# Attention and two MoE layers on one core: tails of four heads in one load, second keys copied on the chip, tails summed in one step

## The chip, the cores and the metric

One core of a Trainium2 chip runs the whole program. The metric is the device time of one execution in microseconds (us); the number quoted is the median of several executions.

## What is computed

The reference is an attention layer, then a top-1 mixture of experts, then a soft mixture. B=4, H=8, S=576, D=64; 2304 tokens of 512 features go through 8 experts of width 1024, twice.

```python
scores = scale * q @ k.T ; causal ; a = softmax(scores) ; local = a @ v
q_p = phi(q)                                  # phi(x) = (x > 0 ? x : exp(x) - 1) + 1
mem_out = (q_p @ M_prev) / (q_p @ z_prev + 1e-6)
attn = g * mem_out + (1 - g) * local          # g = sigmoid(beta), one number a head
logits = x @ w_gate + modality_bias ; e = argmax(logits)
y = gate_w * (relu(x @ w1[e]) @ w2[e])        # then the soft mixture with 32 slots
```

## The kernel before

A head has 576 rows: four chunks of 128 and a tail of 64. The kernel works on 16 pairs p. A pair is the same head of two batches; its two tails of 64 rows share one chunk of 128, chunk 4, so a pair has nine chunks. A head is j = 2p + s, s the place in the pair (0 the even head, 1 the odd one).

Each pair goes through named steps. The names are the ones in the order table at the end of the file, with the line numbers of the profile:

- Loads. `Lk`, `Lq`, `Lv` (L108) load the eight whole chunks of a tensor with two DMAs of 128 KB, issued by SyncE (SP). `Tk`, `Tq`, `Tv` (L113) load the two tails with one DMA of 32 KB, issued by ScalarE (ACT). All goes into `raw`, which has two buffers.
- Splits. Keys, queries, values and phi(q) are split into a high and a low 16-bit part: `kh` (L170 ACT), `kl` (L173 GpSimd), `qh` (L176 ACT), `ql` (L180 VectorE, DVE), `pe` (L184 ACT, an exponential), `prl` (L188 ACT), `pm` (L192 DVE), `ph` (L195 ACT), `pl` (L198 DVE), `vh` (L201 ACT), `vl` (L204 DVE).
- `tr1` (L210, SP): a DMA transpose of keys and queries into `tt`. `k2` (L213, SP): a DMA that copies the high and low keys, 64 partitions x 1152, into `k2t`, of which three buffers are kept; the other 64 partitions hold -1, filled at the start (L121).
- Row maxima. `x0` to `x3` (PE, L225 to L238) multiply the high parts into a PSUM bank `mxp`, and `y0` to `y3` (DVE, L246 and L261) reduce them with the mask added. `x0` of the odd head also does the product of each tail with itself, 64x64, in two products (L230). `tr2` (L265, SP) transposes the maxima and low queries into `q2t`.
- Scores. `S0` to `S3` (PE, L279, L280, L283), then the exponentials `E0` to `E3` (L301 ACT) into `e`, and the low part `el` by `l0` to `l3` (L307 GpSimd). `e` and `el` have two buffers, one for the even and one for the odd head.
- Value sums. `A0` to `A3` (L334 PE) sum a chunk of 128 rows over its key chunks, four products for each (two parts of e by two of v), 65 columns: 64 of values and the row sum. `A4` of each head does the tail: 16 products on 128 rows and, for the tail with itself, four on 64 rows.
- Memory. `M` (L357, L358 PE), `mc`, `mr` (L363, L367 DVE), `mx` (L374 ACT, writes `x_all`). `mL`, `mA` and others prepare the matrices of 8 heads at a time (L151 SP loads `mr`, L157 ACT rounds it to `mh`).
- Norms. `Na` (L384 DVE) takes the row sums of the head's bank; for the odd head a second instruction of one column takes the shared tail, which lies in the even head's bank. `Nb` (L388), `N` (L396 DVE, adds into `x_all`).

The routing of the MoE is worked in chunks among the attention steps: (half, k) with half 0 or 1 and k 0 to 3. `cT` transposes (L551 PE), `cX` copies to SBUF (L558 DVE for g = 1, L560 ACT), `cM` multiplies with the gate weights (L565 PE, one product for each g of 0, 1, 2, into 32 rows of one bank each; float32, two records in the trace for one product), `cC` adds up (L571 or L573 DVE). The last chunk (1, 3) is done in the start of the MoE part (L1176 to L1182). `r1` (L578) and the further steps make the indices. `s00` to `s11` store tokens (L669, L671 SP), `pf` loads the first expert's weights (L1692), `ga` gathers rows (L1695 GpSimd).

The order of all this is written out by hand: `PLACES` gives each step an offset, the period is 10 a pair, pairs 0, 1, 2, 14 and 15 have corrections, and the steps are sorted by `offset + 10 p` and emitted in that order. Each engine runs its instructions in the order in which they were emitted; a wait at one holds all that stand behind it on the same engine.

```python
todo = [(offs[n] + period * p + offs.get(f"{n}@{p}", 0), f"{n}@{p}", lambda f=f, p=p: f(p)) for n, f in steps.items() for p in range(NP)]
todo += [(offs[n], n, f) for n, f in once.items()]
with tc.manual_schedule():
    fills()
    for _, n, f in sorted(todo, key=lambda t: t[:2]):
        f()
```

## Time and profile before

| | us |
|---|---|
| median of three runs | 597.95 |
| lowest and highest run | 597.41, 601.11 |
| profiled execution, its time | 601.41 |
| profiled execution, its span | 599.7 |
| busy in the span: PE, DVE, ACT, GpSimd | 519.3, 347.0, 256.9, 216.7 |

The profiled execution is one run of its own: its time is 3.46 us above the median, and 1.7 us of it lie outside the span that the trace covers. The attention takes up to some 240 us of the span; the rest is the two MoE layers. A busy time counts instructions at work; an engine whose busy share is close to one in a stretch has little room there. Rows with a bracket at the end, `[idle before <-releaser]`, say how long the engine stood idle before the instruction and what released it.

### The profile page before, as it was taken

Reading aid. Unit: us, or ns where it says so; the run is one execution under the profiler, and the core shown is the slowest. Engines: PE = TensorE matmul, PEld = TensorE weight load, DVE = VectorE, ACT = ScalarE, POOL = GpSimd, SP = SyncE. Lnnn points to the kernel's source line nnn. Section 1 sums busy time; section 2 is a strip of 40 time slices with the busy share of each in tenths; the row PEclk is TensorE's granted clock in tenths of the full one; section 3 lists DMA queues with packets and bytes.
Section 4 is the critical chain, followed back from the end, with each engine's and each line's share of the span. In section 5 each row is a group of like instructions: output and inputs, shape, how many; then the busy total and the mean of one; then the engine's idle time right before and its main releaser. Section 6 shows DMA issues by size and latency. Waiting matters only on the chain. (4 is left out here: it accounts for less than half of the span.)

```text
span 599.7 us, 17104 instructions
## 1 busy us (share of the span) xinstructions
PE 519.3 (87%) x6421; PEld 349.4 (58%) x6421; DVE 347.0 (58%) x1194; ACT 256.9 (43%) x580; POOL 216.7 (36%) x277
## 2 busy tenths in 40 slices
PE   0368889999999999659699999998999899789993
PEld 0146656766776868226667667674666567465342
DVE  4668889999988998398542433435443232422233
ACT  4348668777777856252422212423321122210033
POOL 5155656666765757145743210212112111101000
PEclk9998989999999999798899999998999899976998
DMA  5999899999999859893568656761438778585988
GB/s 104 166 175 185 171 183 193 169 175 184 167 165 189 172 120 134 211 213 122 147 192 201 199 178 213 248 179 39 132 91 182 237 235 227 165 314 184 345 261 292
DMA packets 194514, 111.85 MB, mean 187 GB/s; under 512 B 160262, under 2 KB 174543, under 8 KB 194400
## 3 DMA queue, kind: packets, MB, share of 16 engines
q1 hardware_dynamic: 181376, 91.97, 65.7%
q10 hardware_dynamic: 10528, 13.17, 7.7%
q0 software_dynamic: 2496, 5.32, 3.3%
q8 instruction: 54, 0.88, 0.6%
q14 instruction: 60, 0.49, 0.2%
HBM read 75.93 MB, written 9.91 MB: 143 GB/s over the span
## 5 line engine op out<-in xcount | busy, mean ns | idle before, releaser
L307 POOL TENSOR_TENSOR el<-e 128x512 f16<-128x512 f32 (+2 forms) x128 | 113.0, 903 | 71.8 <-ACT e L301 65.3
L1009 PE MATMUL ps_g<-xt,w1h 128*128 128x128 f16 x1088 | 98.7, 221 | 6.0 <-DMA xt<-xt 5.4
L1009 PE MATMUL ps_g<-xt,w1l 128*128 128x128 f16 x544 | 95.2, 221 | 0.2 <-issue 0.2
L1009 PEld LDWEIGHTS <-w1h 128*128 128x128 f16 x1088 | 84.7, 99 | 14.7 <-issue 11.7
L999 PE MATMUL ps_y<-w2h,hts 128*128 128x512 f16 (+1 forms) x288 | 89.2, 377 | 3.2 <-issue 3.2
L301 ACT ACTIVATE e<-sp 128x512 f32<-128x512 f32 (+2 forms) x128 | 62.9, 510 | 43.8 <-PE sp L280 16.5
L1061 POOL DMA_INDIRECT cbuf<-ce,gidx x17 | 17.7, 1042 | 162.1 <-DVEq L1396 89.7
L334 PE MATMUL avp<-vh,e 128*128 128x65 f16 (+2 forms) x480 | 74.4, 199 | 0.3 <-DVE x_all L396 0.3
L334 PE MATMUL avp<-vl,e 128*128 128x65 f16 (+2 forms) x480 | 72.8, 196 | 0.0
L334 PE MATMUL avp<-vl,el 128*128 128x65 f16 (+2 forms) x480 | 72.5, 195 | 0.0
L334 PE MATMUL avp<-vh,el 128*128 128x65 f16 (+2 forms) x480 | 72.2, 194 | 0.0
L334 PEld LDWEIGHTS <-e 128*128 128x128 bf16 (+2 forms) x960 | 62.5, 102 | 16.6 <-issue 10.6
L999 PEld LDWEIGHTS <-hts 128*128 128x128 f16 x432 | 43.4, 104 | 45.0 <-issue 4.0
L279 PE MATMUL sp<-tt 128*128 128x64 f16 (+4 forms) x288 | 59.9, 251 | 2.3 <-ACT e L301 2.2
L334 PEld LDWEIGHTS <-el 128*128 128x128 f16 (+2 forms) x960 | 61.8, 103 | 0.1
L280 PE MATMUL sp<-q2t,k2t 128*128 128x64 f16 (+4 forms) x288 | 57.0, 250 | 3.5 <-DMA q2t<-qs 3.5
L1016 ACT ACTIVATE hts<-ps_g 128x512 f16<-128x512 f32 x34 | 20.3, 597 | 84.6 <-PE ps_g L1009 84.6
L999 PE MATMUL ps_y<-w2l,hts 128*128 128x512 f16 (+1 forms) x144 | 54.1, 376 | 0.0
L1009 PEld LDWEIGHTS <-w1l 128*128 128x128 f16 x544 | 53.7, 99 | 0.0
L246 DVE CUSTOM_DVE_ANT_0 mxp<-mxp,mq 128x512 f32<-128x512 f32 (+1 forms) x64 | 39.5, 626 | 13.6 <-PE mxp L232 8.3
L1036 DVE COPY si<-ps 128x512 f32<-128x512 f32 x19 | 13.1, 689 | 51.7 <-PE ps L1034 51.7
L1017 DVE SCALAR_TENSOR_TENSOR hts<-ps_g,hts 128x512 f16<-128x512 f32 x34 | 23.5, 690 | 33.4 <-ACTq L1377 22.7
(410 smaller groups left out, 1139.4 us busy)
## 6 DMA issues: line engine op xcount, KB each, us to landing
va<-in_moe_w_dram SPq DMA_DIRECT2D x12, 1024.0 KB
va<-in_moe_w_dram ACTq DMA_DIRECT2D x9, 1024.0 KB
rw<-in_moe_w_dram SPq DMA_DIRECT2D x8, 1024.0 KB
va<-in_moe_w_dram SPq DMA_DIRECT2D x16, 512.0 KB
raw<-in_q_dram SPq DMA_DIRECT2D x32, 128.0 KB
raw<-in_k_dram SPq DMA_DIRECT2D x32, 128.0 KB
raw<-in_v_dram SPq DMA_DIRECT2D x32, 128.0 KB
rw<-in_moe_w_dram SPq DMA_DIRECT2D x2, 2048.0 KB
```

What stands on the lines that cost most here:

```text
L246: nc.vector.tensor_tensor_reduce(out=ps[:, src:src + n] if out is None else out, in0=ps[:, src:src + n], in1=msk, scale=1.0, scalar=-3.0e3 ...
L279: nc.tensor.matmul(ps[:, dst:dst + n], k1[:, ko:ko + 128], q1[:, qo:qo + n], start=True, stop=False)
L280: nc.tensor.matmul(ps[:, dst:dst + n], k2[:, ko:ko + 128], q2[:, qo:qo + n], start=False, stop=last)
L301: nc.scalar.activation(out=es[j % 2][0][:, a:a + n], in_=st.pop(("sp", j, g))[:, 0:n], func=AF.Exp, scale=0.125)
L307: nc.gpsimd.tensor_tensor(el[:, a:a + n], e[:, a:a + n], hv[:, a:a + n], op=ALU.subtract)
L334: nc.tensor.matmul(dst, l, r, start=(i == 0), stop=(i == len(mms) - 1))
L999: nc.tensor.matmul(ps, a[:, l, :], r, start=(start and j == 0), stop=(stop and j == 2))
L1009: nc.tensor.matmul(dst, l, r, start=(j == 0), stop=(j == len(mms) - 1))
L1016: nc.scalar.activation(out=hi, in_=ps, func=AF.Relu)
L1017: nc.vector.scalar_tensor_tensor(lo, ps, 0.0, hi, op0=ALU.max, op1=ALU.subtract)
L1036: nc.vector.tensor_copy(st["x2t"], tp)
L1061: ins = nc.gpsimd.indirect_dma_start(out=cbuf, out_offset=bass.IndirectOffsetOnAxis(ap=idx, axis=0), in_=ce, in_offset=None, bounds_check= ...
```

## The change

1. Tails. One load `U` for a tensor brings the tails of four pairs (a group g; two DMAs of 64 KB, issued by SP, with the 64 rows as the leading dimension) into one tile `tls`, which has a single buffer for each tensor. `Tk`, `Tq`, `Tv` become copies on ACT, 128x64, from `tls` into chunk 4 of `raw`. 24 DMAs take the place of 48; 48 copies are new.
2. `k2` becomes a copy on DVE, 64x1152; two buffers of `k2t` in place of three.
3. The two 64x64 tail products of `x0` become one of 128x128, whose mask has the two off-diagonal quarters closed; its reduction has 128 columns in place of 64.
4. `A40` and `A41` become one step `A4` a pair: 20 products for each head, all on 128 rows, the two heads taken in turn into the two halves of the columns, in the odd head's bank. The odd head's `Na` is one instruction in place of two. The even head's `e` and `el` are held until `A4`.
5. The three `cM` products of a chunk are issued behind one another, as one step; the third `xt` lies in a part of another tile.
6. `PLACES` is new throughout. At the start SP's order is `Uq0 Lq0 Lk0 Uk0 Lq1 Lk1 mL0 .. tr1@0 .. tr2@0` (before: `Lq0 Lk0 .. Lk1 Lq1 tr1@0 Lk2 mL0 Lv0 tr1@1 k2@0 Lq2 tr2@0`), and `mA0` stands behind `pe@1` and `kh@2` on ACT (before: ahead of `pe@1`). Pair 0's reductions stand almost together. The loads of group 1 stand behind `Lq4`, those of group 2 behind `Lk8`, `Uv2` ahead of `Lk10`, and those of group 3 around `Lk12`. At the end, the transposes of chunk (1, 2) lie among pair 15's steps, its products behind `A20@15` and its sum behind the last norm `N1@15`.

The diff, with the order table left out:

```diff
@@ -54,10 +54,6 @@
...
     c["mq"] = mq
-    mqt = const.tile([128, 64], BF16, name="mqt")
-    nc.vector.tensor_copy(mqt[0:64], mq[0:64, 384:448])
-    nc.vector.tensor_copy(mqt[64:128], mq[64:128, 448:512])
-    c["mqt"] = mqt
     zero = const.tile([128, 1], BF16, name="zero")
@@ -74,8 +70,9 @@
...
         NP = 16
-        NR, NSRC, NTT, NV, NK2, NQ2 = 2, 2, 5, 5, 3, 3
+        NR, NSRC, NTT, NV, NK2, NQ2 = 2, 2, 5, 5, 2, 3
         raws = [ap.tile([128, 3, 9, 64], F32, name=f"raw{i}") for i in range(NR)]
+        tls = ap.tile([128, 3, 4, 64], F32, name="tl")
         srcs = [ap.tile([128, 27, 128], F16, name=f"src{i}") for i in range(NSRC)]
@@ -86,7 +83,7 @@
...
-        junk = [junk[:, 0:128], junk[:, 128:384], junk[:, 384:448]]
+        junk = [junk[:, 0:128], junk[:, 128:384], junk[:, 384:512]]
         cfm = [ap.tile([128, 5], F32, name=f"cfm{i}") for i in range(2)]
@@ -96,6 +93,8 @@
...
         ml = ap.tile([128, B * H, 65], F16, name="ml")
+        mqt = ap.tile([128, 128], BF16, name="mqt")
         st = {}
@@ -108,11 +107,20 @@
...
-        def load_tails(p, i, t):
-            b0, h = 2 * (p // 8), p % 8
-            nc.scalar.dma_start(out=raws[p % NR][:, i, 4, :], in_=t[b0:b0 + 2, h, 512:576, :])
+        def load_tails(g, i, t):
+            b0, h = 2 * (g // 2), 4 * (g % 2)
+            for s in range(2):
+                nc.sync.dma_start(out=tls[64 * s:64 * s + 64, i], in_=t[b0 + s, h:h + 4, 512:576, :].rearrange("h r d -> r h d"))
+        def put_tails(p, i):
+            nc.scalar.activation(out=raws[p % NR][:, i, 4, :], in_=tls[:, i, p % 4, :], func=AF.Copy)
         def fills():
+            nc.gpsimd.memset(mqt, NEG)
+            for s in range(2):
+                d = slice(64 * s, 64 * s + 64)
+                nc.vector.tensor_copy(mqt[d, d], cs["mq"][d, 384 + 64 * s:448 + 64 * s])
             nc.gpsimd.memset(x_all[0:64, 0, :], 0.0)
@@ -210,7 +218,7 @@
...
         def k_again(p):
-            nc.sync.dma_start(out=k2s[p % NK2][0:64], in_=tts[p % NTT][0:64, 0:9, :])
+            nc.vector.tensor_copy(k2s[p % NK2][0:64], tts[p % NTT][0:64, 0:9, :])
@@ -225,9 +233,8 @@
...
                 if s == 1:
-                    for i in range(2):
-                        t = side(i)[1]
-                        nc.tensor.matmul(ps[64 * i:64 * i + 64, 384:448], q1[:, t:t + 64], k1[:, t:t + 64], start=True, stop=True)
+                    nc.tensor.matmul(ps[:, 384:512], q1[:, 512:640], k1[:, 512:640], start=True, stop=True)
             elif part == 1:
@@ -251,7 +258,7 @@
...
                 if s == 1:
-                    ttr(64, 384, 10, cs["mqt"], junk[2])
+                    ttr(128, 384, 10, mqt, junk[2])
             elif part == 1:
@@ -306,32 +313,33 @@
...
-        def av(j, c):
-            p, s = j // 2, j % 2
+        def av_terms(j, cols, n, base):
             e, el = es[j % 2]
             hv = e.bitcast(BF16).rearrange("p (n t) -> p n t", t=2)[:, :, 1]
-            vh, vl = vhs[p % NV], vls[p % NV]
-            a = j if c < 4 else j - s
-            if c == 0:
-                st["av", j] = ps_a.tile([128, 325], F32, name="avp", tag="av")
-            acc = st["av", a]
-            base = 5 * s
-            if c < 4:
-                cols = [128 * c, 512 + 128 * (c - 1), 960 + 128 * (c - 2), 1280 + 128 * (c - 3)][:c + 1]
-                n, dst = 128, acc[:, 65 * c:65 * c + 65]
-            else:
-                cols = [1472, 896, 1216, 1408, 1536]
-                n, dst = 64, acc[64 * s:64 * s + 64, 260:325]
-            mms = []
+            vh, vl = vhs[j // 2 % NV], vls[j // 2 % NV]
             for kc, a in enumerate(cols):
-                r = slice(0, 128) if kc < 4 else slice(64 * s, 64 * s + 64)
                 ch = base + kc if kc < 4 else 4
...
                     for rh in (vh, vl):
-                        mms.append((lh[r, a:a + n], rh[r, ch, :]))
+                        yield lh[:, a:a + n], rh[:, ch, :]
+        def av(j, c):
+            if c == 0:
+                st["av", j] = ps_a.tile([128, 325], F32, name="avp", tag="av")
+            dst = st["av", j][:, 65 * c:65 * c + 65]
+            cols = [128 * c, 512 + 128 * (c - 1), 960 + 128 * (c - 2), 1280 + 128 * (c - 3)][:c + 1]
+            mms = list(av_terms(j, cols, 128, 5 * (j % 2)))
             for i, (l, r) in enumerate(mms):
                 nc.tensor.matmul(dst, l, r, start=(i == 0), stop=(i == len(mms) - 1))
+        def av_tails(p):
+            acc = st["av", 2 * p + 1]
+            mms = [list(av_terms(2 * p + s, [1472, 896, 1216, 1408, 1536], 64, 5 * s)) for s in range(2)]
+            for i in range(20):
+                for s in range(2):
+                    l, r = mms[s][i]
+                    nc.tensor.matmul(acc[64 * s:64 * s + 64, 260:325], l, r, start=(i == 0), stop=(i == 19))
@@ -374,14 +382,10 @@
...
-        def banks(j):
-            return [(st["av", j], 0, 4)] + ([(st["av", j - 1], 4, 1)] if j % 2 else [])
         def norm_cf(j):
-            h = j // 2 % 8
-            for a, c0, n in banks(j):
-                nc.vector.tensor_scalar(cfa[j % 2][:, c0:c0 + n], wsum(a, 5)[:, c0:c0 + n], 1e-9, c1[:, h:h + 1], op0=ALU.add, op1=ALU.mult)
+            h, n = j // 2 % 8, 4 + j % 2
+            nc.vector.tensor_scalar(cfa[j % 2][:, 0:n], wsum(st["av", j], n), 1e-9, c1[:, h:h + 1], op0=ALU.add, op1=ALU.mult)
@@ -389,17 +393,16 @@
...
-            h = j // 2 % 8
-            for a, c0, n in banks(j):
-                for c in range(c0, c0 + n):
-                    xt = x_all[:, tiles(j, c), 64 * h:64 * h + 64]
-                    nc.vector.scalar_tensor_tensor(xt, a[:, 65 * c:65 * c + 64], cfa[j % 2][:, c:c + 1], xt, op0=ALU.mult, op1=ALU.add)
+            h, a = j // 2 % 8, st.pop(("av", j))
+            for c in range(4 + j % 2):
+                xt = x_all[:, tiles(j, c), 64 * h:64 * h + 64]
+                nc.vector.scalar_tensor_tensor(xt, a[:, 65 * c:65 * c + 64], cfa[j % 2][:, c:c + 1], xt, op0=ALU.mult, op1=ALU.add)
         steps = {"Lk": lambda p: load(p, 0, k), "Lq": lambda p: load(p, 1, q), "Lv": lambda p: load(p, 2, v),
-                 "Tk": lambda p: load_tails(p, 0, k), "Tq": lambda p: load_tails(p, 1, q), "Tv": lambda p: load_tails(p, 2, v),
+                 "Tk": lambda p: put_tails(p, 0), "Tq": lambda p: put_tails(p, 1), "Tv": lambda p: put_tails(p, 2),
                  "kh": k_hi, "kl": k_lo, "qh": q_hi, "ql": q_lo, "tr1": tr1, "pe": phi_e, "prl": phi_r,
                  "pm": phi_m, "ph": phi_hi, "pl": phi_lo, "vh": v_hi, "vl": v_lo, "k2": k_again,
-                 "tr2": tr2}
+                 "tr2": tr2, "A4": av_tails}
         for s in range(2):
@@ -408,7 +411,7 @@
...
                 steps[f"S{i}{s}"], steps[f"E{i}{s}"], steps[f"l{i}{s}"] = head(st_group, i), head(e_exp, i), head(e_lo, i)
-            for i in range(5):
+            for i in range(4):
                 steps[f"A{i}{s}"] = head(av, i)
@@ -417,6 +420,9 @@
...
                 once[f"{n}{i}"] = lambda f=f, i=i: f(i)
+        for g in range(4):
+            for i, (n, t) in enumerate((("k", k), ("q", q), ("v", v))):
+                once[f"U{n}{g}"] = lambda g=g, i=i, t=t: load_tails(g, i, t)
         period, offs = at
@@ -488,6 +494,9 @@
...
         self.place = pool.tile([128, NT, 128], BF16, name="place")
+        self.xt2 = self.place[:, 9:18].rearrange("p a b -> p (a b)").bitcast(F32)
+        self.fo = self.xt2[:, 384:384 + 9 * NE].rearrange("p (t e) -> p t e", e=NE)
+        self.xt2 = self.xt2[:, 0:384]
         self.iop = iof("iop", [128, 1], [[0, 1]], cm=1)
@@ -552,18 +561,19 @@
...
     def chunk_x(self, g):
-        xt = self.st["xt", g] = self.wk.tile([128, 384], F32, name="xt", tag="xt")
+        xt = self.st["xt", g] = self.xt2 if g == 2 else self.wk.tile([128, 384], F32, name="xt", tag="xt")
         xp = self.st.pop(("xp", g))
...
-    def chunk_m(self, k, g, bank):
-        if g == 0:
-            self.st["lp"] = bank()
-        self.nc.tensor.matmul(self.st["lp"][32 * g:32 * g + 32, 0:384], self.wg[:, k, :], self.st.pop(("xt", g)), start=True, stop=True,
-                              tile_position=(0, 32 * g))
+    def chunk_m(self, k, bank):
+        self.st["lp"] = bank()
+        for g in range(3):
+            self.nc.tensor.matmul(self.st["lp"][32 * g:32 * g + 32, 0:384], self.wg[:, k, :], self.st.pop(("xt", g)), start=True, stop=True,
+                                  tile_position=(0, 32 * g))
@@ -694,7 +704,7 @@
...
         sh = [128, 9, NE]
-        o = wk.tile(sh, F32, name="fo", tag="fo", bufs=1)
+        o = self.fo
         s = wk.tile([128, 9], F32, name="fs", tag="fs")
@@ -1176,8 +1186,7 @@
...
                 first_split(0, 0)
-                for g in range(3):
-                    rt.chunk_m(3, g, lambda: rot("ps_y", 2))
+                rt.chunk_m(3, lambda: rot("ps_y", 2))
                 rt.chunk_c(1, 3)
@@ -1710,7 +1719,7 @@
...
                 once[f"cX{half}{k}{g}"] = lambda g=g: rt.chunk_x(g)
-                once[f"cM{half}{k}{g}"] = lambda k=k, g=g: rt.chunk_m(k, g, lp_bank)
+            once[f"cM{half}{k}"] = lambda k=k: rt.chunk_m(k, lp_bank)
             once[f"cC{half}{k}"] = lambda half=half, k=k: rt.chunk_c(half, k)
```

## Rows read from the trace of the kernel before

**Rows 1.** Windows, 75 to 225 us: window, length, busy (x instructions) per engine, PEclk, DMA share, GB/s

```profile
75.00:225.00 150.00, 144.81 (x2405) 104.28 (x2401) 135.75 (x515) 110.72 (x278) 94.05 (x106) 0.99 0.95 172
```

**Rows 2.** DMA view, 75 to 225 us: queues by kind, then issues by line

```profile
q10 hardware_dynamic: 3900, 0.98, 3.2%
...
k2t<-tt SPq DMA_DIRECT2D x12, 144.0 KB
```

**Rows 3.** Waits, PE, 75 to 225 us: us in total, times, longest us

```profile
PE mxp L225 <- DVE qs L246: 2.0, 2, 1.7
```

**Rows 4.** Waits, DVE, 75 to 225 us: the first and last of nine on PE

```profile
DVE R L246 <- PE mxp L230: 2.9, 4, 1.2
...
DVE acc L571 <- PE lp L565: 0.2, 1, 0.2
```

**Rows 5.** Timeline, PE, from 125 us: start us, duration us, instruction

```profile
126.09 0.20 PE L334 MATMUL avp<-vl,e 128*64 128x65 f16 x1
...
126.53 0.20 PE L334 MATMUL avp<-vl,el 128*64 128x65 f16 x1
126.66 0.22 PE L334 MATMUL avp<-vh,e 64*64 64x65 f16 x1
...
126.97 0.27 PE L226 MATMUL mxp<-tt 128*128 128x256 f16 x1
127.17 0.22 PE L230 MATMUL mxp<-tt 128*64 128x64 f16 x2
127.33 0.20 PE L334 MATMUL avp<-vh,e 128*128 128x65 f16 x1
...
131.17 0.22 PE L357 MATMUL mmp<-mh,tt 128*64 128x65 f16 x2
131.22 0.20 PE L358 MATMUL mmp<-ml,tt 128*64 128x65 f16 x2
```

**Rows 6.** Windows, line L565 alone, 75 to 225 us

```profile
75.00:225.00 150.00, 15.65 (x36) 2.52 (x36) 0.99 0.95 172
```

**Rows 7.** Timeline, PE, 245 to 258 us

```profile
251.07 1.29 PE L565 MATMUL ps_y<-xt,wg 128*32 128x384 f32 x4
```

**Rows 8.** Timeline, SP, 120 to 150 us

```profile
120.89 0.52 SPq L213 DMA_DIRECT2D k2t<-tt  x1
```

**Rows 9.** Timeline, DVE, 222 to 300 us

```profile
243.33 0.86 DVE L396 SCALAR_TENSOR_TENSOR x_all<-avp,cfa,x_all 128x64 f32<-128x64 f32 x4 [4.64 <-remote]
...
268.85 0.37 DVE L787 TENSOR_SCALAR R<-R,iop 128x576 bf16<-128x576 bf16 x1
```

**Rows 10.** Groups by shape, 0 to 300 us: busy us, mean ns, idle before

```profile
L374 ACT ACTIVATE x_all<-mmp,cfm 128x64 f32<-128x64 f32 x144 | 32.9, 320 | 9.2 <-DVE cfm L367 8.9
...
L198 DVE TENSOR_TENSOR src<-pm,src 128x576 f16<-128x576 f32 x16 | 17.0, 1062 | 3.6 <-ACT src L195 3.6
...
L246 DVE CUSTOM_DVE_ANT_0 R<-mxp,mq 128x128 bf16<-128x128 f32 x32 | 8.9, 278 | 4.3 <-PE mxp L230 3.6 <-PE mxp L226 0.8
...
L246 DVE CUSTOM_DVE_ANT_0 R<-mxp,mqt 128x64 bf16<-128x64 f32 x16 | 3.5, 218 | 0.0
...
L384 DVE TENSOR_SCALAR cfa<-avp,c 128x1 f32<-128x1 f32 x16 | 3.3, 205 | 0.0
...
L121 DVE MEMSET k2t<- 64x1152 f16 x3 | 3.1, 1018 | 0.7 <-issue 0.5 <-DMA raw<-in_q_dram 0.2
```

**Rows 11.** Timeline, DVE, 0 to 44 us

```profile
25.66 0.76 DVE L198 TENSOR_TENSOR src<-pm,src 128x576 f16<-128x576 f32 x1
```

**Rows 12.** Timeline, PE, 0 to 75 us

```profile
33.34 0.37 PE L280 MATMUL sp<-q2t,k2t 128*128 128x256 f16 x1 [3.46 <-DMA q2t<-qs]
```

**Rows 13.** Timeline, SP, 0 to 44 us

```profile
12.14 2.81 SPq L210 DMA_TRANSPOSE tt<-src  x1
...
29.05 1.30 SPq L265 DMA_TRANSPOSE q2t<-qs  x1
```

**Rows 14.** Timeline, ACT, 0 to 44 us

```profile
22.91 0.64 ACT L157 ACTIVATE mh<-mr 128x520 f16<-128x520 f32 x1 [5.92 <-DMA mr<-in_M_prev_dram]
```

152 lines of the change are left out of this document (76 added, 76 removed).

## The prediction

> **What bounds the kernel now.** I read the page's 40 slices first: the first 16 (attention, up to some 240 us) are where the change lives, TensorE (PE) and VectorE (DVE) both near full there, with the granted clock at its upper level. The expert blocks behind are touched only by their start. So I took the steady middle, 75 to 225 us, as my sample. The reader is to see in [rows 1] that of 150 us PE is busy 144.81, DVE 135.75, ScalarE 110.72 and GpSimd 94.05, and that the DMA engines are 95% taken. Twelve pairs pass in it (12 issues of `k2t` in [rows 2]), so a pair costs 150 / 12 = 12.5 us. Who waits for whom: PE's largest wait for another engine is 2.0 us in all [rows 3], while DVE waits for PE in nine rows, from 2.9 down to 0.2 us, 11.6 us in sum, of its 150 - 135.75 = 14.25 us of idle time [rows 4]. So PE is the bound and DVE is next, about 10% behind. That decides how much of a saving on PE can reach the time: the room to DVE, less what the change gives DVE to do.
>
> **What the change takes from PE.** (a) The tail sums. A tail step of one head is 16 products on 128 rows at 0.031 us ((126.53 - 126.09) / 14), then a change of tile shape (126.53 to 126.66 = 0.13, that is 0.10 more than a product), four 64-row products and another change at its end [rows 5]. Two heads: 40 x 0.031 = 1.24 plus six changes of shape. After: 20 couples in the two halves of the columns and two changes. A couple in two halves starts 0.05 after the one before (131.17 to 131.22, two products each) [rows 5], so 20 x 0.052 = 1.04. Saved: 0.20 + 4 x 0.10 = 0.60 a pair. (b) The tail maxima: from L226 to the next step is 127.33 - 126.97 = 0.36; at 0.031 for 65 columns L226's 256 take 0.12, and one 128-column product in the shape of its neighbours would take 0.06. Saved 0.18. Together 0.78 a pair, 9.4 us in the twelve pairs.
> (c) The routing products. 18 of them (36 records) take 15.65 us, 0.87 each [rows 6]. The change issues the three of a chunk behind one another, into three column groups. Four records that stood together took 1.29 against 2 x 0.87 = 1.74 [rows 7], so they overlap; I take about 0.9 for three adjacent instead of 2.6, the low end, because each goes to its own columns as the couples in (a) do; the high end is 3 x 0.65 = 1.9. Saved 1.65 a chunk (0.7 at the high end), six chunks in the stretch: 9.6 us. PE's load in the stretch falls by 9.4 + 9.6 = 19.0 us. It can't all be had: DVE is 14.25 us away.
>
> **What it gives DVE.** The copy `k2` (64x1152, 16-bit) replaces a DMA issue of 0.52 us on SP [rows 8]. No DVE row shows it. Nearest below: a 128x576 pass of 16-bit data at 0.37 [rows 9], half the columns. Nearest above: the fill of the same tile, 64x1152, at 1.02 [rows 10], plus some 0.3 where it stands against GpSimd, for a pass over 576 columns takes 0.76 with GpSimd idle [rows 11] and 1.06 in the mean of sixteen [rows 10]. Ends 0.37 and 1.3; I take 0.7, twice the 16-bit row, since it is the same kind of pass. The tail maximum grows from 64 to 128 columns: 278 - 218 = 0.06 more; one 128x1 normaliser goes: 0.205 less [rows 10]. Net 0.7 + 0.06 - 0.205 = +0.56 a pair, +6.7 in the stretch: DVE at 135.75 + 6.7 = 142.5 busy. Of its idle time the waits for PE go down with PE's load, which I put at two thirds, 11.6 to 3.9; what else it waits for (14.25 - 11.6 = 2.65) stays. 142.5 + 3.9 + 2.65 = 149.0: **the steady stretch gains only 1 us**, and DVE becomes the bound.
> [...]
>
> **What it moves off the queues.** 48 tail DMAs leave ScalarE's queue (3.2% of the DMA time in the stretch [rows 2]); 48 copies of 128x64 come onto ScalarE. The nearest row, a 128x64 pass that reads PSUM, is 0.32 [rows 10]; 48 x 0.3 = 14 us over all attention, 10 in the stretch: 110.7 + 10 = 121 of 150, hidden beneath PE and DVE as long as nothing on DVE waits for the order of ScalarE (if that cover goes, it is a few tenths a pair). SP loses 16 issues of 0.52 and gets 24 of the kind, +5 us over 240: hidden, but in the start four of these stand ahead of the first transpose. The DMA engines lose the twelve `k2t` transfers and the small tail packets; they were not what PE waited for, so nothing.
>
> **The start.** The first score product waits until 33.34 for `q2t` [rows 12], whose transpose is issued at 29.05 behind the maxima of pair 0 [rows 13]. Between stands a stall: ScalarE idles 5.92 for `mr` before `mh` at 22.91 [rows 14], DVE waits behind it, and the maxima of pair 0 are split around it. After, the `mr` load is issued before pair 0's transpose and the reductions of pair 0 run together, which would end them some 4 us earlier; but four tail DMAs and the `mr` load (together some 2 us) stand ahead of the first transpose, which is issued at 12.14 now. Sum -2, bounds -5 and +2.
>
> **The end.** After the last norm the old order still has routing products, a transposed chunk and the sums on them (rows at 251.07 [rows 7]); in the new order the transposes of the chunk before last lie among the last pair's steps, its products before the last tail sums, and only one sum is behind the last norm. I take 3 products and a copy, -3 (bounds -5, -1.5). The four pairs outside the stretch and the start take a part of the PE saving where DVE is less full: 4 x 0.5 = -2.
>
> **Sum.** -1 - 2 - 3 - 2 = -8 us (stretch, start, end, other pairs). The profiled execution took 601.41, and DVE stood idle 4.64 us before the norm at 243.33 with nothing of its own core named as releaser [rows 9]; I count this as an accident of that execution, neither gained nor lost, and the median 597.95 lies 3.46 below it. From the median: 597.95 - 8 = **590**.
>
> **The rivals.**
> 1. *The copy is cheap and PE's saving comes through* (0.2). With 0.37 a copy DVE's net is +0.23 a pair, 135.75 + 2.7 = 138.5; if its PE waits vanish, 138.5 + 2.65 = 141.1, -8.9 in the stretch, -7 elsewhere: 597.95 - 15.9 = **582**. For it: PE's 19.0 is more than all DVE's idle time. Against: the new order's waits needn't vanish.
> 2. *The copy eats it* (0.17). At 1.3 DVE gets +1.15 a pair, 13.8: 149.6 busy plus 2.65 plus a little, some +3 in the stretch, against -3 at the end and -2 at the start: **596 to 598**. For it: the row at 1.02, and GpSimd busy 94 of 150. Against: 0.37.
> 3. *Slower: the one tail buffer stalls ScalarE* (0.12). All tails of four pairs lie in one tile. The next group's load can't start before the last copy of the group, and the copies of pairs 4, 8 and 12 wait in order on ScalarE until it lands: issue some 1.1 us for the two DMAs and some 2.9 to the data's use (from a transpose's issue to the first product on it passed 33.34 - 29.05 = 4.3, its issue 1.3 of that). Nine such loads at 1.5 us of wait each are +13, with nothing behind ScalarE moving (its exponentials, pe, kh): 597.95 - 8 + 13 = 603, and some of the saving lost to DVE's waits: **604 to 606**. It decides from where ScalarE reaches the copy less than 4 us after SP issued the load. For it: single buffer, DMA engines 95% full. Against: the order puts the loads of group 1 right behind pair 4's own loads, many us ahead of their use.
> A fourth, in the range only: the even head's tail columns are held until the joint tail step, so the next pair's exponentials wait for it. That loop holds GpSimd's passes of a pair, 94.05 / 12 = 7.8, the tail step of some 1.1 and the exponential ahead: some 10 us, below the pair's 12.5; it decides when these grow by 2.5.
>
> **How the numbers follow.** Forecast 0.51 with its own range 585 to 595, rivals 0.2, 0.17 and 0.12. A measurement of this kernel tells about 1% from no change, that is 592 and 604. Faster than 592: four fifths of the forecast, 0.41, and the first rival, 0.2: 0.61. Slower than 604: the third rival, 0.12. The rest, 0.27, between. For eight in ten I go down to 579, a little below the first rival (with the start at its -5), and up to 601, which takes in the second rival with the start at +2 but not the third.
>
> **What would show it.** Right: the same stretch with PE busy at 130 or less, DVE above 95% and its waits for PE well under 11.6, a pair at 12.3 us or just under; L213 on DVE at 0.6 to 0.8; the tail sums as one run of some 1.1 us; three routing products in some 0.9; the first `q2t` transpose near 27; the step to the first block's split some 3 us nearer the last norm. Wrong: L213 at 0.4 with a pair at 11.8 (first rival), or at 1.2 and GpSimd's passes longer (second); ScalarE's waits headed by its tail copies on DMA (third). PE still over 140 would say that the routing products don't overlap, and then the steady gain is gone.

## The result, and the profile after

The changed kernel took 582.82 us (median of four runs, 580.75 to 584.44) against 598.12 before (four runs, 597.41 to 601.11): a ratio of 0.973, 95% interval 0.969 to 0.978. It is faster by 15.3 us where 8 were forecast; the time lies in the range, and the direction is right. The working behind it is right in size in the steady stretch and in direction at the start, wrong at the end of attention, and blind to the part of the kernel that gave two thirds of the gain.

The steady stretch, 75 to 225 us, in the columns of [rows 1], whole and then line L575 alone (the routing products, [rows 6] before):

```profile
75.00:225.00 150.00, 127.53 (x2527) 97.62 (x2522) 141.88 (x538) 116.51 (x316) 103.74 (x109) 0.99 0.94 169
```

```profile
75.00:225.00 150.00, 5.08 (x36) 0.90 (x36) 0.99 0.94 169
```

PE fell from 144.81 to 127.53 busy, DVE rose from 135.75 to 141.88. The granted clock is 0.99 in both; over the first 240 us it was 0.98 in the kernel before and 0.96 in the changed one. Six routing chunks take 5.08 us, 0.85 for three products. The transposes of maxima `q2t` of pairs 4 and 14 tell what a pair takes, ten pairs lying between them; changed kernel, then the kernel before:

```profile
79.26 1.28 SPq L272 DMA_TRANSPOSE q2t<-qs  x1
...
203.36 1.28 SPq L272 DMA_TRANSPOSE q2t<-qs  x1
```

```profile
85.81 1.65 SPq L265 DMA_TRANSPOSE q2t<-qs  x1
...
212.07 1.29 SPq L265 DMA_TRANSPOSE q2t<-qs  x1
```

A pair takes 12.41 us, where it took 12.63 before. The waits of PE and then of DVE in the same stretch (us in total, times, longest), [rows 3, 4] before:

```profile
PE mxp L239 <- DVE qs L268: 6.5, 7, 1.5
```

```profile
DVE mxp L253 <- PE mxp L241: 3.0, 5, 1.0
DVE cfm L371 <- PE mmp L366: 1.1, 2, 0.7
DVE mxp L253 <- PE mxp L239: 1.1, 2, 0.7
```

PE now waits for DVE, 6.5 us in its largest row, where it was 2.0. DVE waits for PE in five rows (the three largest are shown), 6.1 us in sum, where it was 11.6. The groups by shape up to 300 us, [rows 10] before:

```profile
L117 ACT ACTIVATE raw<-tl 128x64 f32<-128x64 f32 x48 | 12.3, 268 | 2.8 <-DMA tl<-in_k_dram 2.0 <-DMA tl<-in_q_dram 0.8
...
L221 DVE COPY k2t<-tt 64x1152 f16<-64x1152 f16 x16 | 9.0, 565 | 1.2 <-DMA tt<-src 1.2
...
L253 DVE CUSTOM_DVE_ANT_0 R<-mxp,mqt 128x128 bf16<-128x128 f32 x16 | 4.6, 285 | 0.0
```

The copy of the keys takes 0.565 us in the mean, the tail copy on ACT 0.268, the wider tail reduction 0.285. The first two transposes in SP's timeline, [rows 13] before:

```profile
12.65 2.90 SPq L218 DMA_TRANSPOSE tt<-src  x1
...
24.96 1.34 SPq L272 DMA_TRANSPOSE q2t<-qs  x1
```

The first `q2t` is issued 4.1 us earlier (29.05 before), though `tt` is issued half a us later.

### The profile page after: what moved, and what is told of

Read it like the earlier page. It is cut to its first block, busy times and chain, and to the rows that moved or that the text cites. A ratio compares the mean times of both kernels' runs of the same rounds, so it can differ in the third digit from the quotient of the medians.

```text
span 582.6 us, 17035 instructions
## 1 busy us (share of the span) xinstructions
PE 485.6 (83%) x6405; PEld 331.5 (57%) x6405; DVE 350.8 (60%) x1193; ACT 262.6 (45%) x628; POOL 224.0 (38%) x278
## 5 line engine op out<-in xcount | busy, mean ns | idle before, releaser
L1009 PE MATMUL ps_y<-w2h,hts 128*128 128x512 f16 (+1 forms) x288 | 86.3, 367 | 2.8 <-issue 2.8
L308 ACT ACTIVATE e<-sp 128x512 f32<-128x512 f32 (+2 forms) x128 | 61.3, 512 | 22.2 <-PE sp L287 10.8
L286 PE MATMUL sp<-tt 128*128 128x64 f16 (+4 forms) x288 | 58.6, 249 | 2.5 <-ACT e L308 2.1
L287 PE MATMUL sp<-q2t,k2t 128*128 128x64 f16 (+4 forms) x288 | 54.5, 249 | 4.6 <-DVE k2t L221 3.0
L333 PEld LDWEIGHTS <-e 128*128 128x128 bf16 x640 | 43.4, 101 | 13.4 <-issue 9.7
L333 PE MATMUL avp<-vh,el 128*128 128x65 f16 x320 | 47.8, 198 | 2.8 <-POOL el L314 2.8
L333 PE MATMUL avp<-vh,e 128*128 128x65 f16 x320 | 48.0, 199 | 1.9 <-DVE x_all L399 1.9
L333 PE MATMUL avp<-vl,e 128*128 128x65 f16 x320 | 47.9, 199 | 0.0
L333 PE MATMUL avp<-vl,el 128*128 128x65 f16 x320 | 47.8, 198 | 0.0
L333 PEld LDWEIGHTS <-el 128*128 128x128 f16 x640 | 41.6, 101 | 3.3 <-POOL el L314 3.2
```

Of the source, the lines that this page charges most:

```text
L286: nc.tensor.matmul(ps[:, dst:dst + n], k1[:, ko:ko + 128], q1[:, qo:qo + n], start=True, stop=False)
L287: nc.tensor.matmul(ps[:, dst:dst + n], k2[:, ko:ko + 128], q2[:, qo:qo + n], start=False, stop=last)
L308: nc.scalar.activation(out=es[j % 2][0][:, a:a + n], in_=st.pop(("sp", j, g))[:, 0:n], func=AF.Exp, scale=0.125)
L333: nc.tensor.matmul(dst, l, r, start=(i == 0), stop=(i == len(mms) - 1))
L1009: nc.tensor.matmul(ps, a[:, l, :], r, start=(start and j == 0), stop=(stop and j == 2))
```

## The experiments

Two more profiles of both kernels came first, beside two mixtures: all parts in the old order, and the new order with the old parts.

**before_again** is the kernel before, unchanged.

> The kernel before, unchanged, for a second profile. The first one stood idle 4.6 us ahead of the last norm (239 to 243) and took 307.9 us from the first expert product to the end, with the granted clock low around 467, 523 and 539. If both are accidents of that execution: no idle time there, and about 300 from the first expert product to the end. If they belong to the kernel: both again, 4 to 5 us and about 308. Time 597 to 601 either way.

596.37 us, ratio to the kernel before 1.002 (0.999 to 1.006). The idle time of 4.64 us ahead of the last norm [rows 9] belongs in part to that one execution: in this profile the norm at the same place waited 2.60 us, for the sums of its own head. The long stretch behind comes again: from the first expert product (274.6) to the end of the span (598.3) it took 323.7 us, with the granted clock at 0.95 over that stretch (0.94 in the first profile, and there 0.85, 0.78 and 0.66 in the 10 us around 467, 523 and 539). (The 307.9 of this expectation and the 299.5 of the next count from a later product, at 291.8 and 283.1, behind the first wait for `xt`; from the first expert product on, the first profiles took 319.0 and 311.5.)

**after_again** is the changed kernel, unchanged.

> The changed kernel, unchanged, for a second profile: 581 to 584.5. The first one took 299.5 us from the first expert product to the end; again 298 to 301 if that stretch is the same in both kernels, and if the one of before above also gives about 300, the 15 us lie ahead of the experts altogether.

580.11 us, 0.974 (0.970 to 0.979). First expert product at 269.8, and 309.4 from there. So the 15 us split into some 4 ahead of the experts (274.6 to 269.8 and 271.1; the 280.7 of the first profile holds the idle time above) and some 11 behind in the mean (319.0 and 323.7 to 311.5 and 309.4), in code that the change doesn't touch.

**order_old**: all parts, the old places, `A4` behind the last low part of the odd head, `U` of a group behind the last tail copy of the group before.

```diff
-Lk -42.822 Tk -38.5829 Uk0 -378.373 Lq -41.3362 Tq -38.3373 Uq0 -493.4126 Lv -16.185 Tv -13.7705 Uv0 -160.6726 kh
...
+Lk -43.1613 Tk -42.3547 Lq -41.5991 Tq -40.4589 Lv -10.956 Tv -9.4604 kh -36.6118 ...
...
+... A4 6.5 ... A4@3 -0.5545 ... Uk1 -11.8547 Uk2 28.1453 ... Uq1 -9.9589 ... Uv1 21.0396 ...
```

> All parts of the change, in the old order (A4 behind the odd head's last low part, each tail load one pair ahead of its first copy). If the parts carry the gain and the order only fits them: PE busy near 128 of 150 in 75 to 225, a pair at 12.4 to 12.6, the start as before (first transpose of maxima near 29), 588 to 593. If the order carries it: 595 to 600. If the tail copies on ScalarE hurt where the order was not made for them: above 600.

584.63 us, 0.981 (0.977 to 0.986), faster than either side expected. PE 127.1 of 150 busy and a pair at 12.46, as expected, the first `q2t` at 26.96 (near 29 was expected), the first expert product at 275.5: **ahead of the experts no gain of the parts alone is seen**, and the 11 us behind came all the same (311.6).

**parts_old**: the new order, the old parts.

```diff
-            nc.vector.tensor_copy(k2s[p % NK2][0:64], tts[p % NTT][0:64, 0:9, :])
+            nc.sync.dma_start(out=k2s[p % NK2][0:64], in_=tts[p % NTT][0:64, 0:9, :])
-            nc.scalar.activation(out=raws[p % NR][:, i, 4, :], in_=tls[:, i, p % 4, :], func=AF.Copy)
+            nc.scalar.dma_start(out=raws[p % NR][:, i, 4, :], in_=t[b0:b0 + 2, h, 512:576, :])
...
```

(with the tail products of a4_apart and the routing products of cm_apart, both below)

> The new order with the old parts: keys copied by DMA (two buffers), tails loaded by ScalarE's queue, tail maxima in two products, the tail sums one head behind the other with the 64-row products, routing products of a chunk apart. If the parts carry the gain: PE busy back to 143 or more, a pair at 12.6 to 13, 592 to 599. If the order carries it: a pair at 12.4, 583 to 587.

659.66 us, 1.107 (1.103 to 1.112): outside what either side expected. A pair took 17.4. ACT's waits in 75 to 225:

```profile
ACT vh L202 <- DMA raw<-in_v_dram: 19.8, 5, 5.7
ACT vh L202 <- issue: 14.7, 3, 5.6
ACT src L171 <- DMA raw<-in_k_dram: 14.1, 8, 2.8
```

ScalarE's splits wait for the loads into `raw`. A likely reading, not tested by itself, is that the new order counts on tails that are there long before their use. The run says nothing on what the parts are worth, only that parts and order belong together.

**before_tails** and **after_dummy** ask whether the 48 small DMAs on ScalarE's queue slow the expert part: in the first profiles with a long expert part that queue took 2.6 to 4.4 us for three weight loads.

```diff
-        NR, NSRC, NTT, NV, NK2, NQ2 = 2, 2, 5, 5, 3, 3
+        NR, NSRC, NTT, NV, NK2, NQ2 = 2, 2, 5, 5, 2, 3
+        tls = ap.tile([128, 3, 4, 64], F32, name="tl")
-            nc.scalar.dma_start(out=raws[p % NR][:, i, 4, :], in_=t[b0:b0 + 2, h, 512:576, :])
+                nc.sync.dma_start(out=tls[64 * s:64 * s + 64, i], in_=t[b0 + s, h:h + 4, 512:576, :].rearrange("h r d -> r h d"))
+            nc.scalar.activation(out=raws[p % NR][:, i, 4, :], in_=tls[:, i, p % 4, :], func=AF.Copy)
...
```

That is before_tails, against the kernel before. after_dummy, against the changed kernel:

```diff
+        dums = [junk[:, 512 + 128 * i:640 + 128 * i].bitcast(F32) for i in range(5)]
+        def put_tails(p, i, t):
...
+            nc.scalar.dma_start(out=dums[(3 * p + i) % 5], in_=t[b0:b0 + 2, h, 512:576, :])
...
```

> The kernel before with the new tails alone (group loads on SP, copies on ScalarE; two buffers of the second keys and one small routing tile laid elsewhere to make room); old order, all else as before. In the profiles so far the stretch from the first expert product to the end took 319.0 and 323.7 us in the kernel before, 311.5 and 309.4 in the changed one, 311.6 with all parts in the old order, though no code of it changed; in the slow ones ScalarE's queue takes 2.6 to 4.4 us to issue three weight loads that take 0.95 in the others, PE waits there, and the granted clock falls after it. Theory A: the 48 small tail DMAs that ScalarE's queue has carried make its later issues slow. Then here 309 to 312 for that stretch, the three issues in about 1 us, and 584 to 589 in all. Theory B: it comes with PE's load in attention or with the moment at which the experts begin: then 319 to 324 and 594 to 599.

597.09 us, 1.003 (0.998 to 1.008); 320.5 us from the first expert product on, which comes at 274.4, as in the kernel before: in the old order no gain of the new tail loads is seen, and no cost of two buffers of `k2t` in place of three.

> The changed kernel, with the 48 old tail DMAs of 32 KB issued on ScalarE's queue besides, into room that nobody reads. Theory A: from the first expert product to the end 317 to 324 us, the three weight issues at 2.6 us or more, 588 to 596 in all. Theory B: 309 to 312 for that stretch and 580 to 585 in all (attention may pay a little for 48 issues of 0.5 us on ScalarE).

596.10 us, 1.001 (0.997 to 1.005); but 309.2 us from the first expert product on. Theory A falls twice: the expert part is long without these DMAs and short with them. The price of after_dummy lies in attention, whose first expert product comes at 288.7, some 18 later. PE's largest wait and the wait of the copies, 75 to 225:

```profile
PE mxp L244 <- DMA tt<-src: 11.9, 6, 4.7
```

```profile
ACT raw L120 <- DMA R<-in_q_dram: 5.5, 4, 2.5
```

The second row belongs to the experiment (five places for 48 loads, each load waits for an earlier one into its place), so the 18 us are no clean price of 48 DMAs. What is seen of them is PE's wait of 11.9 us for `tt`, which was 1.8 and 1.1 in two rows of the changed kernel.

**k2_dma** is the first line pair of parts_old alone, on the changed kernel.

> The changed kernel with the second keys copied by SP's DMA again, two buffers, same order. The copy takes 0.565 us of VectorE a pair. If VectorE bounds the steady stretch (the forecast): a pair 0.3 to 0.5 shorter, 575 to 579, unless SP, which now stands at the copy until the transpose has landed, delays the transposes of maxima behind it: then 582 to 590. If PE's waits or the DMA set the pair: no change, 579 to 582.

590.52 us, 0.994 (0.990 to 0.999), slower than the changed kernel (0.973 and 0.974), and as short behind, 308.7. The window, then PE's largest wait:

```profile
75.00:225.00 150.00, 123.48 (x2407) 93.79 (x2408) 135.04 (x505) 112.78 (x304) 95.86 (x103) 0.98 0.98 176
```

```profile
PE mxp L241 <- DMA tt<-src: 8.3, 5, 2.5
```

DVE is relieved of 7 us, PE waits 8.3 us for the transposes `tt` instead, and a pair takes 13.0 us. The first expert product is at 277.9, 7 to 8 later. So in the new order the copy on DVE is no price: it pays. How the DMA costs this isn't shown. That SP, standing at the copy, holds up the transposes behind it is not borne out by SP's waits: at the copy it stands 4.4 us in the stretch, for PE, and at the transposes `tt` 43 us with the DMA and without it, for other engines. The DMA engines are 98% busy here, 94 and 96% in the changed kernel; a slower landing is a rival that no run tests by itself.

**cm_apart**: the three products of a chunk with other products between them (2 units of the order apart, less where the sum follows soon).

```diff
-            once[f"cM{half}{k}"] = lambda k=k: rt.chunk_m(k, lp_bank)
+            for g in range(3):
+                once[f"cM{half}{k}{g}"] = lambda k=k, g=g: rt.chunk_m(k, lp_bank, (g,))
...
```

> The changed kernel with the three routing products of a chunk issued apart, other products between them. PE gets 3 x 0.87 in place of 0.85 a chunk, 1.75 more, 12 us in seven chunks. If VectorE bounds the pair (the forecast), most of this fills PE's idle time: 581 to 585. If PE's work still counts in full: 589 to 592.

579.84 us, 0.976 (0.971 to 0.982): no difference from the changed kernel. The window, whole and then the routing products alone:

```profile
75.00:225.00 150.00, 133.56 (x2505) 99.07 (x2504) 141.73 (x543) 116.35 (x316) 104.78 (x110) 0.99 0.91 168
```

```profile
75.00:225.00 150.00, 12.51 (x36) 2.08 (x36) 0.99 0.91 168
```

PE has 6.0 us more to do in the stretch (133.56 against 127.53) and it costs nothing: PE doesn't bound this stretch any more. But 6.0 us are 1.0 a chunk, and 1.75 was expected: apart, the products take 12.51 / 18 = 0.70 each here and not 0.87, and lie in part beside others.

**after_shifted** and **before_moved** ask for the layout: the change took a mask of 128 bytes out of the constants, so every tile of the expert part lies 128 bytes earlier.

First after_shifted, against the changed kernel, then before_moved, against the kernel before:

```diff
+    pad = const.tile([128, 64], BF16, name="pad128")
+    nc.vector.memset(pad, 0.0)
...
```

```diff
-    mqt = const.tile([128, 64], BF16, name="mqt")
...
+        mqt = ap.tile([128, 64], BF16, name="mqt")
...
```

> The changed kernel with 128 unused bytes a partition among the constants, so that all tiles of the expert part lie 128 bytes further on, where they lie in the kernel before (the change moved the tail mask, 128 bytes then, out of the constants); a small start tile is laid into another to make room. Theory L (the layout of the expert part makes the difference in it): 317 to 324 us from the first expert product to the end, 590 to 596 in all. Theory P (the parts of attention make it, through what they leave behind): 309 to 312, 579 to 583.

577.68 us, 0.970 (0.965 to 0.974); 308.5 us from the first expert product on.

> The kernel before, with its tail mask among attention's own tiles, so that the tiles of the expert part lie where they lie in the changed kernel; nothing else. Theory L: 309 to 312 us from the first expert product to the end, 583 to 588 in all. Theory P: 319 to 324, 594 to 597.

600.68 us, 1.007 (1.003 to 1.011); 319.3. The layout of the expert part is not what makes it long. (The total lies 4 above the range; the first expert product came at 283.4, 9 later than in before_again. Why isn't shown.)

**a4_apart**: the old tail products on the changed kernel.

```diff
-                    nc.tensor.matmul(ps[:, 384:512], q1[:, 512:640], k1[:, 512:640], start=True, stop=True)
+                    for i in range(2):
+                        t = side(i)[1]
+                        nc.tensor.matmul(ps[64 * i:64 * i + 64, 384:448], q1[:, t:t + 64], k1[:, t:t + 64], start=True, stop=True)
-                    ttr(128, 384, 10, mqt, junk[2])
+                    ttr(64, 384, 10, mqt, junk[2])
-            for i in range(20):
-                for s in range(2):
+            for s in range(2):
+                for i in range(20):
                     l, r = mms[s][i]
+                    if i > 15:
+                        l, r = l[64 * s:64 * s + 64], r[64 * s:64 * s + 64]
...
```

> The changed kernel with the old tail products on TensorE: two 64x64 tail maxima and a reduction over 64 columns, the tail sums one head behind the other with four products on 64 rows. Layout of the expert part as in the changed kernel. By the forecast's working TensorE gets 0.78 us a pair more and VectorE 0.06 less; TensorE had 150 - 127.5 = 22 us idle in 75 to 225, so most is covered: attention longer by 0 to 4, and by theory L 309 to 312 from the first expert product on, 579 to 585 in all. If the old tail products are what makes the expert part long: 317 to 324 there and 588 to 595 in all.

593.01 us, 0.997 (0.992 to 1.001), and both halves of the expectation are seen:

```profile
75.00:225.00 150.00, 139.94 (x2557) 108.29 (x2555) 143.23 (x548) 118.22 (x319) 102.28 (x109) 1.00 0.97 171
```

PE has 12.4 us more to do in the stretch, 1.03 a pair, and attention is not longer than in the changed kernel (first expert product at 270.8). But from there to the end it takes 318.9 us.

What do the long ones have in common? The page counts PE's products. It shows 6405 for the changed kernel, 6421 for a4_apart:

```profile
PE 485.6 (83%) x6405; PEld 331.5 (57%) x6405; DVE 350.8 (60%) x1193; ACT 262.6 (45%) x628; POOL 224.0 (38%) x278
```

```profile
PE 506.4 (86%) x6421; PEld 348.6 (59%) x6421; DVE 349.0 (59%) x1193; ACT 262.8 (45%) x628; POOL 222.0 (38%) x277
```

| kernel | PE products | first expert product at | from there to the end |
|---|---|---|---|
| before, before_again | 6421 | 280.7, 274.6 | 319.0, 323.7 |
| before_tails, before_moved | 6421 | 274.4, 283.4 | 320.5, 319.3 |
| parts_old, a4_apart | 6421 | 343.2, 270.8 | 317.3, 318.9 |
| after, after_again | 6405 | 271.1, 269.8 | 311.5, 309.4 |
| order_old, after_dummy | 6405 | 275.5, 288.7 | 311.6, 309.2 |
| k2_dma, cm_apart | 6405 | 277.9, 266.9 | 308.7, 309.4 |
| after_shifted | 6405 | 266.2 | 308.5 |

The 16 are the second tail product of `x0` of each pair. The third column also shows how far attention scatters: after_shifted and cm_apart, and after_split below (265.5), which differ little from the changed kernel or give PE more to do, get to the experts 3 to 6 us ahead of it. Two readings of the long expert part are left: the number itself, or the old tile shapes. **after_split** adds 16 products without these shapes.

```diff
-                    nc.tensor.matmul(ps[:, 384:512], q1[:, 512:640], k1[:, 512:640], start=True, stop=True)
+                    for i in range(2):
+                        nc.tensor.matmul(ps[:, 384 + 64 * i:448 + 64 * i], q1[:, 512:640], k1[:, 512 + 64 * i:576 + 64 * i], start=True, stop=True)
```

> The changed kernel with its 128x128 tail maximum issued as two products of 64 columns each, full tiles, same result: 16 products and 16 weight loads more on TensorE, about 0.03 us each, and no change of tile shape. So far every kernel with 13610 to 13615 instructions in TensorE's program took 308.5 to 311.6 us from the first expert product to the end, and had no idle time of kind issue at the start of the soft mixture; every kernel with 13643 to 13648 took 317 to 324 and stood idle there for 1.2 to 3.9 us with nothing named that it waited for, the granted clock low for some 16 us after. This one has 13643. Theory I (the length of TensorE's program ahead of that place decides): idle time of kind issue there, 317 to 321 from the first expert product on, 588 to 594 in all. Theory T (the 64-row and 64-column tile shapes, or the busier attention, decide): no such idle time, 308 to 312, 578 to 582 in all.

585.73 us, 0.985 (0.978 to 0.991), between the ranges of the two theories: 2.9 and 5.6 above the two medians of the changed kernel, whose intervals (up to 0.978 and 0.979) touch this one, so the times alone hardly tell them apart. Attention is as short as in any kernel (first expert product at 265.5), and from there it takes 316.1, outside the 308.5 to 311.6 of the seven with 6405 products.

```profile
PE 483.0 (83%) x6421; PEld 331.1 (57%) x6421; DVE 352.4 (61%) x1193; ACT 262.2 (45%) x628; POOL 219.3 (38%) x278
```

One place that differs is the start of the soft mixture, in PE's timeline: kernel before (before_again), changed kernel (after_again), a4_apart, after_split:

```profile
531.46 0.30 PE L1458 MATMUL ps_g<-idf,dpn 128*32 128x128 f32 x1
535.29 0.31 PE L1458 MATMUL ps_g<-idf,dpn 128*32 128x128 f32 x1 [3.53 <-issue]
```

```profile
521.43 0.44 PE L1452 MATMUL ps<-idf,x 128*128 128x128 f32 x2 [0.56 <-DVE al L1090]
521.80 0.41 PE L1467 MATMUL ps_g<-idf,dpn 128*32 128x128 f32 x2
```

```profile
524.80 0.44 PE L1455 MATMUL ps<-idf,x 128*128 128x128 f32 x2 [0.57 <-DVE al L1093]
526.66 0.41 PE L1470 MATMUL ps_g<-idf,dpn 128*32 128x128 f32 x2 [1.43 <-issue]
```

```profile
517.32 0.44 PE L1453 MATMUL ps<-idf,x 128*128 128x128 f32 x2 [0.57 <-ACT x L1442]
521.22 0.41 PE L1468 MATMUL ps_g<-idf,dpn 128*32 128x128 f32 x2 [3.45 <-issue]
```

The same products, on the same data. In the changed kernel the second row starts 0.4 us after the first; in the other three PE stands idle for 1.4 to 3.5 us ahead of it or in it, and the profile names "issue", that is, nothing that it waited for. Now the windows, in the same sequence; first from the first expert product to the end, then 16 us around the place (the PEclk column is the third from the end):

```profile
274.60:598.30 323.70, 288.89 (x3021) 189.41 (x3019) 119.76 (x341) 81.51 (x172) 61.61 (x75) 0.95 0.67 200
530.60:546.60 16.00, 11.98 (x71) 8.08 (x75) 4.41 (x23) 2.21 (x8) 0.98 (x1) 0.65 0.68 258
```

```profile
269.80:579.20 309.40, 281.05 (x3021) 185.58 (x3019) 119.60 (x341) 81.58 (x172) 61.36 (x75) 0.97 0.68 210
521.40:537.40 16.00, 15.67 (x149) 8.05 (x153) 5.52 (x25) 2.87 (x10) 1.49 (x2) 1.00 0.91 325
```

```profile
270.80:589.70 318.90, 289.43 (x3021) 190.68 (x3019) 119.84 (x342) 81.61 (x172) 62.07 (x75) 0.94 0.65 204
525.00:541.00 16.00, 14.57 (x86) 8.65 (x88) 4.48 (x22) 2.18 (x9) 1.26 (x2) 0.57 0.54 200
```

```profile
265.50:581.60 316.10, 283.63 (x3021) 186.34 (x3019) 119.63 (x341) 81.58 (x172) 62.30 (x75) 0.95 0.66 205
520.50:536.50 16.00, 15.07 (x117) 7.73 (x121) 3.98 (x19) 1.71 (x7) 0.98 (x1) 0.79 0.58 216
```

In the 16 us the granted clock is 1.00 in this profile of the changed kernel and 0.57 to 0.79 in the others, where PE was idle just before. The clock there doesn't tell the two kinds apart by itself, for the first profile of the changed kernel has 0.79 without such an idle time, as much as after_split:

```profile
520.10:536.10 16.00, 14.83 (x106) 7.52 (x109) 4.26 (x21) 2.19 (x9) 2.37 (x3) 0.79 0.75 279
```

Over the whole stretch before_again has 288.89 - 281.05 = 7.8 us more busy time than after_again for the same 3021 records, and 34.8 - 28.35 = 6.5 us more idle time: there the loss is in both, idle time, and the same products at a lower clock (0.95 against 0.97). after_split has 1.0 and 2.6 us more busy time than the two profiles of the changed kernel and 3.6 and 4.1 us more idle time: its loss is mostly idle time.

Nor is it all at this place. Some 70 us ahead of it a product waits for VectorE, behind an exponential of ScalarE, which stands until ScalarE's queue has issued three weight loads (those of before_tails' expectation). From the first of the three issues to the end of the last passed 2.61 us in the first profile of the kernel before, 4.43 in before_again, 1.65 in after_split and 1.45 in the first profile of the changed kernel, where the last two alone took 0.95; in after_split the last one ends at 449.86 and the exponential starts at 449.96. PE's wait in after_split, then in after_again:

```profile
451.74 0.63 PE L1106 MATMUL ps<-dg,onesf 32*128 32x32 f32 x2 [3.35 <-DVE al L1095]
```

```profile
455.78 0.40 PE L1105 MATMUL ps<-dg,onesf 32*128 32x32 f32 x2 [2.09 <-DVE al L1094]
```

In the four profiles of before, before_again, before_tails and before_moved this wait is 3.37 to 6.38 us, in the seven with 6405 products 2.07 to 2.34, but in a4_apart and parts_old only 2.08 and 2.37. Counted in products from the first expert product on, the 1800th to the 2100th, which lie around it, take 32.0 to 36.1 us in those four and 33.0 in after_split, 29.1 to 29.4 in the other nine profiles. The 2500th to the 2600th, around the start of the soft mixture, take 16.3 to 18.6 us in all seven long ones and 12.7 to 14.6 in all seven short ones. So of what after_split loses some 4 us come at the weight loads and some 3 at the start of the soft mixture, and only the latter goes with the 16 products in every profile. The granted clock behind the wait was 0.83 from 468 to 478 us in the first profile of the kernel before, and 1.00 from 456 to 466 in that of the changed one. What delays the weight loads isn't shown.

## Why the prediction was right, and where it was wrong

**The steady stretch: right in size, in part by luck.** Forecast 149.0 / 12 = 12.42 us a pair, measured 12.41 and 12.46, where the kernel before took 12.63 and 12.51. That is 0.6 to 2.6 us in twelve pairs, 1 forecast; the profiles resolve it no better, for cm_apart, after_shifted and after_split have 12.18 to 12.25. PE's load fell by 17.3 us (forecast 19.0), but two terms were off and made up for each other. Undone, the tail products give back 1.03 a pair, 12.4 us, where 0.78 and 9.4 stood (a4_apart). The routing products give back 1.0 a chunk, 6.0 us, where 1.65 and 9.6 stood (cm_apart; and six times 1.65 are 9.9): together they take 0.85, close to the 0.9 taken, but apart they don't cost PE 0.87 each. The copy came to 0.565, between the ends 0.37 and 1.3 and nearest to the 0.7 taken; DVE rose by 6.1 (forecast 6.7), and its waits for PE fell to 6.1 and 4.0 (forecast 3.9). PE's saving is indeed not had in time: with 6.0 us or 12.4 us of it given back (cm_apart, a4_apart) attention was no longer.

**The copy was weighed the wrong way round.** I counted it as a load on DVE and its DMA as free. k2_dma shows that with the DMA in its place the new order is 7 to 8 us longer up to the experts. "They were not what PE waited for, so nothing" fails there: with PE relieved it does wait, 8.3 us for `tt`. In the kernel before PE's waits in the stretch, 2.0 us at most in a row [rows 3], have none on `tt`; whether its greater load hid one isn't shown, and in the old order no gain of dropping the DMA is seen (order_old).

**The start: right way, undersized.** -2 forecast; the first `q2t` came 4.1 and 3.9 earlier (24.96 and 24.87 against 29.05 and 28.73). At pair 15 it is 8.9 and 6.6 (214.46, 214.07 against 223.39, 220.66).

**The end: wrong sign.** -3 forecast, for work that no longer stands behind the last norm. That part is true: from the last norm to the transposes of the logits the kernel before takes 247.0 - 241.4 = 5.6, the changed one 244.2 - 240.9 = 3.3. But the last pair itself became longer. DVE's last norms, before_again and then the changed kernel:

```profile
238.39 0.86 DVE L396 SCALAR_TENSOR_TENSOR x_all<-avp,cfa,x_all 128x64 f32<-128x64 f32 x4 [2.60 <-PE avp L334]
...
240.33 1.05 DVE L396 SCALAR_TENSOR_TENSOR x_all<-avp,cfa,x_all 128x64 f32<-128x64 f32 x5
```

```profile
237.31 0.23 DVE L388 TENSOR_SCALAR cfa<-avp,c 128x5 f32<-128x5 f32 x1 [6.23 <-PE avp L342]
...
239.90 1.04 DVE L399 SCALAR_TENSOR_TENSOR x_all<-avp,cfa,x_all 128x64 f32<-128x64 f32 x5
```

The changed kernel waits 6.23 us for the joint tail step, and its last norm ends 240.94 - 214.46 = 26.5 us after the last `q2t`, in the kernel before 241.38 - 220.66 = 20.7. In after_again the wait is 4.55 and the distance 24.6. I had priced the wait that the tail step puts on the next pair, and not the one at the last pair, where there is no next pair to fill it. Sum of the end: +1.6 to +3.5, not -3. That the joint tail step is what makes it longer is read from this wait; no run undoes it alone.

**The experts: not looked at.** "The expert blocks behind are touched only by their start" is the step that failed, and it is worth 11 of the 15 us. Of the changes, the merged tail maximum takes 16 products from PE's program, and with them goes an idle time some 300 us behind the last of them. Shown is that 16 more products of an ordinary shape bring this idle time back (1.2 to 3.9 us in all seven profiles that have them, 3 to 4 us with what follows) and a stretch of 316.1 against 308.5 to 311.6, and that neither the tail DMAs, nor the layout, nor the order, nor the key copy, nor the routing products alone make the expert part long. The rest of the 11 us is open: 3 to 7 us come at the weight loads, in five of the seven long profiles, and a4_apart, where they cost nothing, still takes 318.9. With one profile of each variant I don't say what is the shapes' part. Why PE stood idle there isn't shown: the profile names no releaser for it.

**The sum: in the range by luck.** Ahead of the experts -8 was forecast and some -4 came, behind them nothing was forecast and some -11 came. The 582.82 lies in the wide range of 579 to 601, but outside the 585 to 595 that the forecast's own working gave.

**The rivals.** The first gave the number (582), but not by its mechanism: the copy is not at 0.37, DVE still waits 6.1 us for PE, and ahead of the experts some 4 us came where it took all of its 15.9. The second is out. The third, the tail buffer, was worth two waits of 0.8 us in ACT's list for the stretch:

```profile
ACT raw L117 <- DMA tl<-in_q_dram: 0.8, 1, 0.8
ACT raw L117 <- DMA tl<-in_k_dram: 0.8, 1, 0.8
```

The idle time at 243.33 was rightly left out of the sum: 2.60 of its 4.64 us are there in the second profile too, and the median moved little (596.37).

## What to carry to other kernels

When an engine is relieved and the time hardly moves in that stretch, undo each part alone on the new kernel: here the part counted as a cost (the copy) paid, and two parts counted as savings (tail products, routing products) paid nothing in the stretch where they stand. A busy time that falls as forecast doesn't prove its terms: here two wrong ones made up for each other. Compare the stretches that a change doesn't touch as well: with a few instructions fewer ahead an idle time far behind was gone, and only a table over all runs, by a count on the profile's page, found it. Then cut such a stretch in pieces, in every profile: the place found first was not the only one, and the low clock behind it (0.79 over 16 us) stood in a profile without the idle time too. A second profile of the kernel before costs little, and tells an accident from a property before a sum is built on it.

## What was not expected of the hardware

Idle time named "issue" of 1.2 to 3.9 us at one place of PE's program, present in all seven profiles with 6421 products, where the seven with 6405 have 0.9 at most. It goes with 16 products more or less ahead of it in the program; what lies between isn't shown. An idle time of the same name stands in all fourteen, 2.8 to 3.3 us, some 11 to 12 us ahead of that place, so the name alone is no sign of a long kernel. Nor is the granted clock behind the place: 0.57 to 0.79 over the 16 us in the seven long ones, 0.79 to 1.00 in the seven short ones.

The copy on DVE takes 0.44 us where GpSimd is idle and up to 1.19 beside one of GpSimd's `el` passes. DVE's copies and GpSimd's passes, changed kernel:

```profile
62.33 1.19 DVE L221 COPY k2t<-tt 64x1152 f16<-64x1152 f16 x1
...
99.75 0.44 DVE L221 COPY k2t<-tt 64x1152 f16<-64x1152 f16 x1
...
122.35 0.45 DVE L221 COPY k2t<-tt 64x1152 f16<-64x1152 f16 x1
```

```profile
61.67 1.54 POOL L314 TENSOR_TENSOR el<-e 128x448 f16<-128x448 f32 x1 [0.79 <-ACT e L308]
...
97.42 1.79 POOL L181 TENSOR_TENSOR src<-raw,src 128x576 f16<-128x576 f32 x1
...
120.39 3.55 POOL L181 TENSOR_TENSOR src<-raw,src 128x576 f16<-128x576 f32 x1
```

At 62.33 GpSimd was at work until 63.21, and the copy took 1.19; at 99.75 GpSimd had ended at 99.21, and it took 0.44. At 122.35 the copy lies inside a pass of GpSimd and still takes 0.45; there the pass is the longer one, 3.55 us where the same pass at 97.42 took 1.79. So a pass of GpSimd beside the copy goes with a longer copy at 62.33 and not at 122.35, and GpSimd's spans are rough. Eleven of the sixteen copies took 0.44 or 0.45 us, so the order of this kernel seldom lets the two meet to the copy's cost, and the mean is 0.565.
